# Attention over a small state and a feed-forward block on one core: two weight sums by one group of matmuls, in a newly written order

## The chip, the cores and the metric

The kernel runs on one core of one Trainium2 chip. The engines named here are PE (TensorE, matmul; its weight loads are shown as PEld), DVE (VectorE), ACT (ScalarE), POOL (GpSimd), and SP (SyncE, which here issues most transfers). The time is that of the device for one execution, in microseconds (us).

## The reference

There are eight batches. In each, eight heads of 512 tokens attend to 32 states (and the states to the tokens), and the 512 + 32 rows that result go through a normalisation and a feed-forward block of width 2048 with a residual.

```python
scores = scale * x @ state.T        # softmax over the 32 states
xread  = a @ state                  # 512 rows a batch and head
scores2 = scale * state @ x.T       # softmax over the 512 tokens
sread  = a2 @ x                     # 32 rows a batch and head
x  = concat(xread, sread) with heads joined   # 8 x 544 x 512
xn = (x - mu) / sqrt(var + 1e-6) * g_ln
out = x + max(xn @ w_ch1, 0) @ w_ch2          # 512 -> 2048 -> 512
```

All is float32. The kernel splits each factor into a high and a low float16 part and adds three products of parts (`TERMS`).

## The kernel before

**Front.** The weights come in float64 words and are turned into float32 by `words` (an ACT step, then two DVE steps for each half). `weights1(u)`, for four units of 512 hidden columns, takes the gain and the mean into the first matrix (`means` is line 600, on PE), finds its size, and writes high and low parts (`w1c`). `weights2(u)` does the second matrix (`w2h`). `attention(b)` loads a batch, scales and splits it (`x16`, `sh`), transposes it by transfers of SP (`xT`, `sT`), and makes scores in two PSUM banks named `banks`; ACT takes exponentials of them (`eB`), and DVE transposes them into `ts` for the other softmax. `state_products(b)` multiplies the state with `w1c` (line 666) into `matrix`.

**Batch 0** runs with plain products: `first_products` (line 702) and `second_products_by_unit` (line 716), while the second weights still arrive.

**Batches 1 to 7** use a form of Strassen's scheme with seven products for eight, which is why sums of weight blocks are needed. `sums_of_weights(u)` works by halves of a unit, two a unit, eight in all. In a half it makes four sums: t3 = b22 − b12, b12 = b12 − b11, t2 = b22 − b12 (the new one) and n4 = b21 − t2. Each is four matmuls with plus and minus unit matrices (line 748, `signs`) into a quarter kilobyte of columns, an ACT copy to the high part, and a DVE subtract for the low part. The first two sums go to the left and right half of one PSUM bank (`acc`), the other two to another bank. A bank that is being read by one engine is not written by another: matmuls that come later in the order than a copy out of that bank wait for the copy.

For each batch, two groups of 256 tokens and four units, `strassen_hidden` makes 2 x 256 hidden columns: for block 1 and block 0 each, 12 matmuls (`first`, line 794) into a bank named `half`, of which there are two, and then ACT and DVE steps that take the positive part and form sums (`rs`, `xs`). Block 0's `rs` sums need the values of block 1. POOL makes low parts of the sums. `strassen_products` then issues four runs of matmuls (line 850) that add up in four `acc` banks over the units, and `together` joins them with ACT, DVE and POOL and stores them. The state rows of all batches go last, as a ninth batch with plain first products (line 803).

**What sets the order.** Each of these generators gives a stream, a list of steps. `PLAN` is a string of items `stream:step`, written out by hand as one long table, and `issue` carries the steps out in just that order: every engine has its instructions in the order of the table, and waits are put in by what a step reads and writes. In the profile nearly all steps of ACT, DVE and POOL carry line 187, which is the line of `do` that calls the instruction, so groups are told apart by the names of tiles.

## Time and profile before

| | |
|---|---|
| median of three runs | 695.02 us (693.15 to 695.36) |
| the profiled execution | 693.68 us |
| its span | 691.9 us |
| PE busy | 633.4 us, 92% of the span |
| DVE, ACT, POOL busy | 498.7, 387.9, 215.9 us |
| granted PE clock, mean | 0.977 |

The span runs from the first to the last instruction; 1.8 us of the execution lie around it. Shares are means over unlike stages: in the first 60 us PE is busy less than half, and DVE nearly always; from 180 us on it is the reverse. Rows of the profile read: line, engine, operation, output <- inputs, shapes, count; then busy time, the mean of one in ns, and the idle time of that engine just before these instructions, with what ended it.

### The profile page before, as it was taken

Reading aid. Unit: us, or ns where it says so; the run is one execution under the profiler, and the core shown is the slowest. Engines: PE = TensorE matmul, PEld = TensorE weight load, DVE = VectorE, ACT = ScalarE, POOL = GpSimd, SP = SyncE. Lnnn points to the kernel's source line nnn. Section 1 sums busy time; section 2 is a strip of 40 time slices with the busy share of each in tenths; the row PEclk is TensorE's granted clock in tenths of the full one; section 3 lists DMA queues with packets and bytes.
Section 4 is the critical chain, followed back from the end, with each engine's and each line's share of the span. In section 5 each row is a group of like instructions: output and inputs, shape, how many; then the busy total and the mean of one; then the engine's idle time right before and its main releaser. Section 6 shows DMA issues by size and latency. Waiting matters only on the chain.

```text
span 691.9 us, 14637 instructions
## 1 busy us (share of the span) xinstructions
PE 633.4 (92%) x5945; PEld 494.0 (71%) x5948; DVE 498.7 (72%) x1002; ACT 387.9 (56%) x699; POOL 215.9 (31%) x189
## 2 busy tenths in 40 slices
PE   0648897989998999999999998999999999999996
PEld 0224554546986798778877987688868877889885
DVE  4999886467666676878787777776787687646733
ACT  5498797465654565556555654475456554435332
POOL 0002242330422332533423342433444233423322
PEclk9979898999999999999999999999999999999999
DMA  8898868125340344134213330453223503144221
GB/s 326 273 253 227 245 170 163 24 39 127 95 67 17 81 124 72 38 91 139 58 47 77 95 56 20 101 135 68 64 65 110 105 1 74 39 108 77 63 63 30
DMA packets 98563, 69.63 MB, mean 101 GB/s; under 512 B 72704, under 2 KB 90624, under 8 KB 98048
## 3 DMA queue, kind: packets, MB, share of 16 engines
q1 hardware_dynamic: 96384, 64.77, 36.9%
q0 software_dynamic: 864, 3.15, 2.4%
q8 instruction: 46, 0.75, 0.5%
q10 hardware_dynamic: 1248, 0.79, 0.4%
q14 instruction: 21, 0.17, 0.1%
HBM read 28.05 MB, written 9.44 MB: 54 GB/s over the span
## 4 chain that ended last, share of the span: by engine, by line
PE 74%; DVE 14%; ACT 7%; DMA 2%; issue 2%; POOL 0%; ACTq 0%; DVEq 0%
PE acc L850 34%; PE half L794 18%; PE acc L716 5%; PE half L666 4%; PE half L803 3%; DVE rs L187 2%; PE acc L748 2%; PE acc L702 2%; PE acc L600 2%; ACT xs L187 2%; DVE w_t L187 2%; ACT sums L187 1%; DVE ts L187 1%; ACT eB L187 1%; DMA w1c<-sums 1%
## 5 line engine op out<-in xcount | busy, mean ns | idle before, releaser
L850 PEld LDWEIGHTS <-xs 128*128 128x128 f16 x2520 | 243.2, 98 | 43.3 <-issue 14.0
L187 POOL TENSOR_TENSOR xs<-rs,xs 128x512 f16<-128x512 f32 x120 | 140.3, 1181 | 270.6 <-ACT xs L187 206.9
L850 PE MATMUL acc<-w2h,xs 128*128 128x256 f16 x1440 | 184.1, 274 | 0.0
L794 PE MATMUL half<-ea,matrix 128*128 128x256 f16 x1344 | 162.7, 273 | 6.1 <-DVE matrix L187 2.7
L794 PEld LDWEIGHTS <-matrix 128*128 128x128 f16 x1344 | 130.2, 98 | 26.0 <-issue 8.0
L850 PE MATMUL acc<-sums,xs 128*128 128x256 f16 x1080 | 141.6, 273 | 0.0
L187 DVE SCALAR_TENSOR_TENSOR rs<-half,rs 128x256 f32<-128x256 f32 x224 | 89.9, 419 | 34.4 <-ACT xs L187 14.7
L187 ACT ACTIVATE xs<-half 128x256 f16<-128x256 f32 (+1 forms) x112 | 54.0, 487 | 89.3 <-DVE rs L187 39.0
L187 ACT ACTIVATE xs<-rs 128x512 f16<-128x512 f32 (+1 forms) x128 | 77.6, 619 | 41.3 <-DVE rs L187 37.5
L187 DVE SCALAR_TENSOR_TENSOR xs<-half,xs 128x256 f16<-128x256 f32 (+1 forms) x112 | 61.1, 550 | 32.4 <-ACT xs L187 30.5
L187 ACT ACTIVATE matrix<-half,hs 128x512 f16<-128x512 f32 x56 | 37.7, 684 | 30.4 <-PE half L666 30.2
L187 DVE SCALAR_TENSOR_TENSOR matrix<-half,hs,matrix 128x512 f16<-128x512 f32 x56 | 41.0, 742 | 15.3 <-ACT matrix L187 15.3
L716 PE MATMUL acc<-w2h,hid 128*128 128x512 f16 x192 | 43.1, 379 | 0.0
L187 DVE TENSOR_TENSOR strip<-acc,strip 128x256 f32<-128x256 f32 (+1 forms) x60 | 33.3, 555 | 11.8 <-PE acc L850 8.0
L187 ACT ACTIVATE rs<-half 128x256 f32<-128x256 f32 x56 | 21.3, 380 | 31.2 <-PE half L794 19.4
L666 PE MATMUL half<-w1c,sT 128*32 128x512 f16 x448 | 33.8, 384 | 2.5 <-DVE xs L187 1.2
L716 PEld LDWEIGHTS <-hid 128*128 128x128 f16 x192 | 18.5, 98 | 22.3 <-issue 1.9
L600 PE MATMUL acc<-w_t,gm 128*128 128x512 f32 x32 | 18.2, 725 | 15.7 <-DVE w_t L187 15.7
L187 POOL TENSOR_TENSOR hid<-strip,hid 128x512 f16<-128x512 f32 x16 | 19.8, 1244 | 39.5 <-ACT hid L187 39.4
L187 POOL TENSOR_TENSOR ts<-ts,mA 128x1024 f32<-128x1024 f32 (+1 forms) x8 | 15.4, 1919 | 51.5 <-DVE of_weights L187 30.1
L702 PE MATMUL acc<-ea,matrix 128*128 128x256 f16 x192 | 26.9, 301 | 2.1 <-ACT strip L187 1.1
L187 POOL TENSOR_TENSOR ts<-ts,dA 128x1024 f32<-128x1024 f32 (+1 forms) x8 | 14.4, 1806 | 45.3 <-DVE of_weights L187 23.6
(152 smaller groups left out, 783.0 us busy)
## 6 DMA issues: line engine op xcount, KB each, us to landing
raw<-in_moe_w_ch_dram SPq DMA_DIRECT2D x9, 1024.0 KB, 10.4
out_dram<-xr SPq DMA_DIRECT2D x16, 512.0 KB, 3.2
x_f<-in_x_dram SPq DMA_DIRECT2D x15, 512.0 KB, 5.6
sums<-in_moe_w_ch_dram SPq DMA_DIRECT2D x7, 1024.0 KB, 6.1
ek<-ea SPq DMA_DIRECT2D x56, 64.0 KB, 2.1
ek<-ek SPq DMA_DIRECT2D x7, 512.0 KB, 4.3
xr<-part POOLq DMA_DIRECT2D x6, 512.0 KB, 5.0
w1c<-raw SPq DMA_DIRECT2D x8, 256.0 KB, 4.2
```

Of the source, the lines that this page charges most:

```text
L187: return lambda: f(*map(now, args), **{k: now(v) for k, v in kw.items()})
L600: nc.tensor.matmul(ps, lhsT=gm[:, k:k + 1].broadcast_to([P, P]), rhs=t4[:, k], start=k == 0, stop=k == 3)
L666: nc.tensor.matmul(ps[32 * j:32 * j + 32], lhsT=sT[:, g, a, 32 * j:32 * j + 32], rhs=w[:, 2 * g + j // 2, j % 2], start=a == 0, stop=a == ...
L702: nc.tensor.matmul(o[:, 256 * f:256 * f + 256], lhsT=m[:, g, i, P * (q + f):P * (q + f) + P], rhs=ea[:, s, k, g], start=f == 0 and g == 0 ...
L716: nc.tensor.matmul(po, lhsT=hid[:, i, q, c * P:(c + 1) * P], rhs=w[:, j, q], start=first and q == 0 and n == 0, stop=last and q == 3 and n ...
L748: nc.tensor.matmul(o, lhsT=signs[:, k // 2], rhs=v[k], start=start and k == 0, stop=k == 3, skip_group_check=True)
L794: nc.tensor.matmul(ps[:, 256 * q:256 * q + 256], lhsT=m[:, h, i, P * (2 * k + q):P * (2 * k + q) + P], rhs=ea[:, 0, j, h, 256 * g:256 * g ...
L803: nc.tensor.matmul(ps[:, 256 * q:256 * q + 256].rearrange("p (t n) -> p t n", t=2), lhsT=w[:, k // 2, k % 2, fs] if k < H else wn[:, k - H ...
L850: nc.tensor.matmul(po[o], lhsT=y[:, n, i, o] if o < 2 else x[:, o - 2, n, i], rhs=v[j], start=u == 0 and n == 0 and k == 0 and o in (2, 1, ...
```

## The change

Two things change. `sums_of_weights` issues the first two sums of a half as one group of eight matmuls; then come their two ACT copies and two DVE subtracts. The third and fourth sum are as they were. The number of instructions on each engine stays the same. Second, `PLAN` is a new table: everything is put in a new order. A further stream, `warmth`, has no steps, since `WARM` is 0.

```diff
+WARM = 0
 PLAN = (
-    "1:2 0:0 1:1 1:0 1:3-15 1:24-25 3:1 3:6 3:5 3:7 1:17-18 1:22 3:0 3:3 1:72 3:2 3:4 3:8 2:1 2:6 2:5 1:23 2:7 1:19 "
...
+    "1:0 1:3-4 1:1-2 1:5-12 4:1 1:19 1:72 0:0 4:6 1:20 1:24-25 4:5 4:7 4:0 4:3 1:17-18 4:2 4:4 3:1 3:6 1:22-23 "
...
-            for k, (d, a, b) in enumerate(((t3, b22, b12), (b12, b12, b11), (t2, b22, b12), (n4, b21, t2))):
-                yield do(subtract, k % 2 == 0, o[k], *a, *b)
-                yield do(nc.scalar.activation, d[0], o[k], AF.Copy)
-                yield do(nc.vector.tensor_tensor, d[1], o[k], d[0], ALU.subtract)
+            for pairs in (((t3, b22, b12), (b12, b12, b11)), ((t2, b22, b12),), ((n4, b21, t2),)):
+                first = len(o)
+                def subtract_all(*v, first=first):
+                    for k in range(len(v) // 5):
+                        subtract(first != 1 and k == 0, *v[5 * k:5 * k + 5])
+                todo = [(d, a, b, o.pop(0)) for d, a, b in pairs]
+                yield do(subtract_all, *[v for d, a, b, p in todo for v in (p, *a, *b)])
+                for d, a, b, p in todo:
+                    yield do(nc.scalar.activation, d[0], p, AF.Copy)
+                    yield do(nc.vector.tensor_tensor, d[1], p, d[0], ALU.subtract)
...
+    warm = half()
+
+    def warmth():
+        for _ in range(WARM):
+            yield do(nc.tensor.matmul, warm, lhsT=ones, rhs=ones.unsqueeze(1).broadcast_to([P, 4, P]), start=True, stop=True)
+
+    streams.append(list(warmth()))
```

ACT's order at the first sums (`sums<-acc` and `w2h<-acc` are the copies of a sum out of its bank, `sums,of_weights<-w_t` the sizes of the last second weights; `part` and `strip` belong to batch 0). Before:

```order
L187 ACTIVATE part<-acc,of_unit 128x512 x2
L187 ACTIVATE strip<-acc 128x512
L187 ACTIVATE hid<-strip 128x2x256
L187 ACTIVATE sums<-acc 128x256
L187 ACTIVATE sums,of_weights<-w_t 128x2048
L187 ACTIVATE sums<-acc 128x256
L187 ACTIVATE w2h<-acc 128x256
L187 ACTIVATE sums<-acc 128x256
```

Now:

```order
L186 ACTIVATE w2h<-acc 128x256
L186 ACTIVATE x_401<-x_f,x_s 128x8x64
L186 ACTIVATE sums<-sums 128x1024
L186 ACTIVATE part<-acc,of_unit 128x512 x2
L186 ACTIVATE sums<-acc 128x256
L186 ACTIVATE x_401<-x_f,x_s 128x8x64
L186 ACTIVATE part<-acc,of_unit 128x512
L186 ACTIVATE sums,of_weights<-w_t 128x2048
L186 ACTIVATE strip<-acc 128x512 x2
```

The first half's two copies (here the second sum's first) now stand ahead of the sizes, with other work between them; before, the second sum of the next half came behind the sizes.

DVE's order at the softmax of batch 2, before:

```order
L187 SCALAR_TENSOR_TENSOR xs<-half,xs 128x2x256
L187 SCALAR_TENSOR_TENSOR rs<-half,rs 128x256 x3
L187 TENSOR_REDUCE mB<-banks 128x2
L187 SCALAR_TENSOR_TENSOR xs<-half,xs 128x2x128
L187 TENSOR_SCALAR mB<-mB,es 128x2
L187 STREAM_TRANSPOSE ts<-banks 128x1024
L187 SCALAR_TENSOR_TENSOR matrix<-half,hs,matrix 128x512
L187 TENSOR_REDUCE mA<-ts 128x32
```

Now:

```order
L186 SCALAR_TENSOR_TENSOR xs<-half,xs 128x2x128
L186 TENSOR_SCALAR es<-x_i 128x1
L186 STREAM_TRANSPOSE ts<-banks 128x1024
L186 SCALAR_TENSOR_TENSOR rs<-half,rs 128x256 x3
L186 SCALAR_TENSOR_TENSOR xr<-strip,of_second,xr 128x512
L186 SCALAR_TENSOR_TENSOR rs<-half,rs 128x256
L186 SCALAR_TENSOR_TENSOR xs<-half,xs 128x2x256
L186 TENSOR_REDUCE mB<-banks 128x2
L186 TENSOR_SCALAR mB<-mB,es 128x2
L186 TENSOR_REDUCE mA<-ts 128x32
```

The transpose `ts<-banks` moved from behind the maxima `mB` (and so behind the exponentials that need them) to ahead of them.

ACT's order in a hidden step of batch 2, with the numbers of the tiles (`half` with the shape 128x2x256 is block 0; 128x256 and 128x2x128 are block 1). Before:

```order
L187 ACTIVATE xs_2746<-half_2724 128x2x128
L187 ACTIVATE rs_2761<-half_2724 128x256
L187 ACTIVATE xs_2746<-half_2748 128x2x256
L187 ACTIVATE xr_2786<-banks_2769,ux_2109 128x1024
L187 ACTIVATE xs_2746<-rs_2761 128x4x128 x2
```

Now:

```order
L186 ACTIVATE xs_2723<-half_2710 128x2x256
L186 ACTIVATE xs_2666<-rs_2633 128x4x128
L186 ACTIVATE rs_2740<-half_2727 128x256
L186 ACTIVATE xs_2723<-half_2727 128x2x128
L186 ACTIVATE xs_2723<-rs_2740 128x4x128 x2
```

Block 0 is now made and read first, and its bank `half_2710` is read again by the `rs` sums once block 1 has been read. In 22 of the 60 hidden steps block 0 comes first now; in 6 of 60 before.

240 rows, old and new, of the table PLAN are left out of this document.

## The prediction

> **What bounds the kernel now.** I read the head and the chain of waits of the profile page first:
>
> ```profile
> span 691.9 us, 14637 instructions
> PE 633.4 (92%) x5945; PEld 494.0 (71%) x5948; DVE 498.7 (72%) x1002; ACT 387.9 (56%) x699; POOL 215.9 (31%) x189
> PE 74%; DVE 14%; ACT 7%; DMA 2%; issue 2%; POOL 0%; ACTq 0%; DVEq 0%
> ```
>
> TensorE (PE) is busy for 633.4 us of 691.9. The change issues the same matmuls, so it can win or lose only in the other 58.5 us and in the time that matmuls take under a lower clock. Where the idle time lies is told by the view of windows (us of the stretch, then busy time and instructions of PE, weight loads, DVE, ACT and POOL, then granted PE clock, DMA share, GB/s):
>
> ```profile
> 0.00:60.00 60.00, 29.17 (x184) 12.96 (x187) 47.86 (x87) 37.22 (x51) 2.80 (x8) 0.89 0.91 276
> 60.00:100.00 40.00, 35.64 (x281) 22.39 (x280) 35.64 (x67) 35.16 (x50) 12.44 (x10) 0.91 0.73 202
> 100.00:160.00 60.00, 52.05 (x340) 28.82 (x339) 38.23 (x67) 39.03 (x66) 18.61 (x16) 0.94 0.42 91
> 160.00:180.00 20.00, 19.53 (x208) 15.45 (x207) 14.54 (x39) 12.51 (x30) 2.27 (x2) 1.00 0.63 159
> 180.00:680.00 500.00, 491.15 (x4888) 409.40 (x4886) 358.77 (x742) 263.07 (x505) 176.82 (x151) 1.00 0.31 72
> 680.00:692.00 12.00, 5.87 (x54) 5.01 (x52) 3.65 (x6) 0.93 (x2) 2.94 (x3) 0.93 0.16 44
> ```
>
> Idle PE time is 30.8 us before 60, 4.4 in 60 to 100, 7.95 in 100 to 160, 0.5 to 180, 8.85 in the 500 us after that, and 6.1 at the end. So the front is where time lies open; the seven batches behind it run PE at 98%. The groups by line say what ended those gaps (busy us, mean ns, then idle before it and its releasers):
>
> ```profile
> L600 PE MATMUL acc<-w_t,gm 128*128 128x512 f32 x32 | 18.2, 725 | 15.7 <-DVE w_t L187 15.7
> L748 PE MATMUL acc<-w2h,signs 128*128 128x256 f16 x112 | 17.3, 288 | 8.4 <-ACT sums L187 4.4 <-DVE sums L187 4.0
> L794 PE MATMUL half<-ea,matrix 128*128 128x256 f16 x1344 | 162.7, 273 | 6.1 <-DVE matrix L187 2.7 <-DVE xs L187 2.1 <-DVE rs L187 0.9
> L666 PE MATMUL half<-w1c,sT 128*32 128x512 f16 x448 | 33.8, 384 | 2.5 <-DVE xs L187 1.2 <-DVE rs L187 1.1
> L850 PE MATMUL acc<-w2h,xs 128*128 128x256 f16 x1440 | 184.1, 274 | 0.0
> ```
>
> The final products (L850) never wait. The mean-taking matmuls (L600) wait 15.7 us for DVE to make weight words, the block sums (L748) 8.4, and the hidden products and state products (L794, L666) 8.6 for one of the two `half` banks. These three rows are what a new order can touch.
>
> **Term A, the merged sums.** Before, each of eight halves takes four turns of a group of four matmuls, an ACT copy and a DVE subtract; now the sums t3 and b12, which share a PSUM bank, are one group of eight. Matmuls, copies and subtracts stay in number (128, 32, 32), so nothing in busy time moves. What goes is a wait inside the bank. The timeline of PE before shows it (start, length, last the idle time and its releaser):
>
> ```profile
> 112.25 1.36 PE L702 MATMUL acc<-ea,matrix 128*128 128x256 f16 x11
> 113.46 0.60 PE L748 MATMUL acc<-w2h,signs 128*128 128x256 f16 x4
> 117.48 1.87 PE L748 MATMUL acc<-w2h,signs 128*128 128x256 f16 x8 [3.42 <-ACT sums L187]
> 119.82 1.01 PE L748 MATMUL acc<-w2h,signs 128*128 128x256 f16 x4 [0.47 <-ACT sums L187]
> 120.62 2.77 PE L702 MATMUL acc<-ea,matrix 128*128 128x256 f16 x12
> 130.91 0.60 PE L748 MATMUL acc<-w2h,signs 128*128 128x256 f16 x4 [1.58 <-DVE sums L187]
> 149.32 0.60 PE L748 MATMUL acc<-w2h,signs 128*128 128x256 f16 x4 [2.41 <-DVE sums L187]
> ```
>
> and the timeline of ACT, why the first is so long:
>
> ```profile
> 114.82 0.37 ACT L187 ACTIVATE sums<-acc 128x256 f16<-128x256 f32 x1
> 115.16 1.91 ACT L187 ACTIVATE sums<-w_t 128x2048 bf16<-128x2048 f32 x1
> 117.07 0.36 ACT L187 ACTIVATE sums<-acc 128x256 f16<-128x256 f32 x1
> ```
>
> The first sum was in its bank at about 114; ACT reached its copy at 117.07, behind the 1.91 us of weight sizes, and the second group, whose matmuls go to the other half of that bank, stood behind that copy. I laid the written order beside these times: each of the four waits (3.42 + 0.47 + 1.58 + 2.41 = 7.88) is a second sum behind the copies of the first. The same four are nearly all of the 7.95 us that PE idles in 100 to 160. As one group both sums lie in the bank before anyone reads it, so this wait cannot occur again; late copies then delay only their own readers: the third sum, which needs the new b12, and the products much later. The ACT order in the change puts the 1.91 us of sizes behind the first such copy (the rows above the prediction), which leaves the third and fourth sums and the banks as the next to be late. There are four `acc` banks, and a later copy holds one longer; at the rate of one group per 1.36 to 2.8 us of other matmuls the next free bank comes about when it is wanted. I take −7.0: the 8.4 less 1.4 for new, short waits of the later sums, three like the 0.47 row. Bounds: −8.4 (all), and −4.4 (only the share that the row puts on ACT, if the DVE lateness shows again at the next reader).
>
> **Term B, the clock behind that gap.** The same PE rows show matmuls at half speed behind the 3.42 us gap: 12 of L702 took 2.77 where 11 took 1.36 before it.
>
> ```profile
> 116.70:123.60 6.90, 5.65 (x28) 3.50 (x31) 1.18 (x3) 1.61 (x6) 0.28 (x1) 0.52 0.46 90
> ```
>
> The granted clock there is 0.52. The loss is 2.77 − 12 × 0.124 = 1.28 on L702, 1.87 − 2 × 0.60 = 0.67 and 1.01 − 0.60 = 0.41 on L748: 2.4 us. Without the gap it isn't paid. I take −2.0, bounds −2.4 and 0 (if another gap as long stands elsewhere in the new order). [...]
>
> **Term C, the order in the batches.** There, three gaps are worth naming; the largest:
>
> ```profile
> 214.64 1.47 PE L794 MATMUL half<-ea,matrix 128*128 128x256 f16 x12
> 216.85 1.25 DVE L187 STREAM_TRANSPOSE ts<-banks 128x1024 f32<-128x1024 f32 x1 [2.88 <-ACT eB L187]
> 218.03 0.71 DVE L187 SCALAR_TENSOR_TENSOR matrix<-half,hs,matrix 128x512 f16<-128x512 f32 x1
> 218.79 2.20 PE L794 MATMUL half<-ea,matrix 128*128 128x256 f16 x12 [2.02 <-DVE matrix L187]
> 220.78 2.46 PE L850 MATMUL acc<-w2h,xs 128*128 128x256 f16 x12
> ```
>
> DVE's transpose of the scores stood 2.88 us for ACT's two exponentials on the same two banks, and behind it in DVE's order stood the `matrix` subtract that frees the `half` bank of the next product. PE paid 2.02, and then 2.20 − 1.47 = 0.73 and 2.46 − 1.47 = 0.99 at the lower clock: 3.7 us. In the new order of batch 2 the transpose stands ahead of the exponentials. Against this, the transpose in batch 4 now stands behind them, which it did not. The rest is how much PE work lies between two uses of a `half` bank. Its release takes, from these rows,
>
> ```profile
> L187 ACT ACTIVATE xs<-half 128x512 f16<-128x512 f32 x56 | 33.2, 594 | 47.9 <-DVE rs L187 24.1 <-PE half L794 18.5 <-PE acc L850 3.8
> L187 DVE SCALAR_TENSOR_TENSOR rs<-half,rs 128x256 f32<-128x256 f32 x224 | 89.9, 419 | 34.4 <-ACT xs L187 14.7 <-ACT rs L187 12.6 <-PE half L794 4.6
> L187 DVE SCALAR_TENSOR_TENSOR xs<-half,xs 128x512 f16<-128x512 f32 x56 | 38.3, 685 | 17.6 <-ACT xs L187 17.6
> ```
>
> for the second-written block three `rs` steps and one `xs` step of DVE, 3 × 0.42 + 0.69 = 1.95, with the 0.59 of ACT ahead 2.5 us. Pricing the matmuls that lie between two uses in the written orders by the means above, 21 of 174 reuses had under 2.5 us of cover and 11 have it now (under 3 us: 35, now 25). By that ratio half of the 8.6 us of waits would go, −4; but 22 of 60 hidden steps, before 6, now compute the block first whose values depend on the other one, so that its bank is held longer, and nothing in the trace prices that at 16 more places. I take −2, the middle of −8 (all 8.6 gone but for the odd one) and +4 (half as much again as there is).
>
> **Term D, the front.** Its end is set by DVE, not by PE:
>
> ```profile
> 7.75 0.17 DVE L187 TENSOR_SCALAR gm<-gx 128x4 f32<-128x4 f32 x1 [5.91 <-DMA gx<-in_moe_g_ln_dram]
> 18.03 4.50 PE L600 MATMUL acc<-w_t,gm 128*128 128x512 f32 x6 [7.12 <-DVE w_t L187]
> 21.23 1.87 SPq L187 DMA_TRANSPOSE sT<-sh  x1
> 41.27 5.68 PE L600 MATMUL acc<-w_t,gm 128*128 128x512 f32 x8 [8.61 <-DVE w_t L187]
> 60.00:80.00 20.00, 16.01 (x162) 11.40 (x161) 19.69 (x39) 19.13 (x27) 6.47 (x5) 0.90 0.91 255
> ```
>
> The move of `gm` off the head of DVE's order lets the work on x start before the 5.91 us wait for gx is over. I followed the chain through the new order with these durations: about 1.5 us earlier for the scale of x; two weight loads swap places, so that the third mean (41.27) can come 2 to 3 us earlier; the transposed x and state are issued behind more of the weights' DVE work, sT at about 22.4 for 21.2, and SP's next weight load, queued behind that transpose, 1.4 us later. Up to the first product DVE has 59.3 us of work ahead of it, before 54.6; up to the first product of the second half of batch 0 both have 99.8. Since DVE is busy 19.69 of 20 us in 60 to 80, a shuffle of equal work there can't win much. I take 0, with −4 (gx and the mean both pass through) and +5 (the 4.7 us more DVE work ahead of the first product stays).
>
> **Term E, a short cover.** One final product of batch 1 now has 1.8 us of work between the steps that make its inputs and itself (2.46 at least before); L850, which waited 0.0, may wait there. +1, bounds 0 and +2. The tail (6.1 us idle in the last window) has the same steps in both, DVE's strips and the last stores: 0.
>
> **The sum.** −7 − 2 − 2 + 0 + 1 = −10. The profiled execution took 693.68 us (span 691.9 and 1.8 around it), so the changed kernel, profiled, should take about 683.7. The median of the three runs shown, 695.02, lies 1.34 above the profiled one; with that, **685 us**.
>
> **The rivals.**
>
> *Nothing gained.* The gaps of 100 to 160 are only where PE meets a front that ACT and DVE feed; close them and PE waits for the next weights instead. For it: ACT and DVE are each busy 35 of 40 us in 60 to 100. Against it: in 160 to 180 PE is busy 19.53 of 20, so work was ready behind the sums, and the feeding engines are busy only 39 and 38 of 60 us in 100 to 160. Time: A and B fall away, C and E nearly cancel: 694.
>
> *Slower by the held banks.* If each of the 16 more steps with the dependent block first holds its bank over the other block's group and its first ACT and DVE steps (1.47 + 0.38 + 0.42 = 2.3 us) and 1.3 of that shows, it costs 16 × 1.3 = 21 us; with A, B, and E, −8 + 21 = +13, less the 4 of the shorter covers: +9, 704. It decides from the point where less than 2.5 us of other PE work lies behind such a pair. Against it: by the written order every such pair but one has 2.6 us or more behind it.
>
> *Slower by the front.* The first product comes 4.7 us later, and with it everything; the sums then find ACT still as busy and A is worth nothing: −2 + 5 + 1 = +4, 699. For it speaks the 19.69 of 20; against it that the work ahead of the second half is equal.
>
> *More than forecast.* The front's 2 to 3 us come through and all of the `half` waits go: A −8.4, B −2.4, C −8, D −3 gives −22, and half of C's remainder lost again, −18: 677.
>
> **How the numbers follow.** Forecast 0.50, nothing gained 0.14, held banks 0.10, late front 0.08, more than forecast 0.18. A change under 0.3% (2.1 us, what the three runs' spread lets one tell) counts as none: that is 692.9 to 697.1. Faster: 0.50 + 0.18 and a small share of "nothing gained", 0.70. Slower: 0.10 + 0.08 = 0.18. Same: 0.12. The forecast's own range by the bounds of A to E, not all at their ends, is 679 to 690. For 8 in 10 I reach down to 675, past most of the large gain, and up to 698, over "nothing gained" and a part of the late front.
>
> **What would show it.** A: the group of L748 (new line) with idle under 2 us in place of 8.4, and PE busy over 57 of 60 us in 100 to 160 of the new profile, or wherever the sums then lie. B: no stretch of clock near 0.5 around the sums. C: idle before L794 and L666 together near 6, no DVE transpose that waits near 3 us in batch 2. D: the first wait of DVE no longer for gx, the third mean near 38 to 39, the first product no later than before. If idle before L794 and L666 is over 15, the held banks decided; if the first products of batch 1 begin later than before, the front did. The forecast is wrong above all if PE's idle time before 180 stays near 43.6 us though the sums no longer wait.

## The result, and the profile after

The changed kernel takes 667.86 us (median of four runs, 667.4 to 668.16); the kernel before, run beside it, 694.85 (693.15 to 695.36). The ratio is 0.9615, with a 95% interval of 0.9597 to 0.9633: 27 us faster, where the prediction had 10 and a range down to 675.

The head of the page and the chain of waits after:

```profile
span 665.9 us, 14680 instructions
PE 626.3 (94%) x5948; PEld 493.1 (74%) x5948; DVE 498.0 (75%) x1002; ACT 388.2 (58%) x699; POOL 216.7 (33%) x189
PE 90%; DVE 5%; DMA 2%; ACT 1%; issue 1%; DVEq 0%; SPq 0%
```

The span is 26.0 us shorter. DVE, ACT and POOL do what they did, to within 1 us. PE's busy time fell by 7.1 us, though its matmuls are the same, and its idle time by 18.9 (58.5 to 39.6); what the 7.1 are is worked out under term B below. The chain that ended last now lies on PE for 90%, before for 74%. Where the idle time went is told by windows cut alike in both. Before:

```profile
0.00:100.00 100.00, 64.81 (x462) 35.34 (x466) 83.49 (x152) 72.37 (x100) 15.24 (x18) 0.90 0.84 246
100.00:180.00 80.00, 71.58 (x546) 44.27 (x545) 52.77 (x105) 51.54 (x95) 20.89 (x18) 0.96 0.48 108
180.00:660.00 480.00, 471.15 (x4705) 391.47 (x4703) 351.51 (x728) 255.96 (x492) 172.32 (x147) 1.00 0.32 73
```

After:

```profile
0.00:100.00 100.00, 68.12 (x502) 38.37 (x503) 84.07 (x154) 74.13 (x104) 15.00 (x19) 0.90 0.83 247
100.00:180.00 80.00, 80.00 (x655) 53.80 (x654) 59.14 (x129) 58.96 (x112) 25.07 (x22) 1.00 0.51 106
180.00:660.00 480.00, 478.12 (x4795) 400.88 (x4793) 352.72 (x717) 255.13 (x484) 176.63 (x148) 1.00 0.31 75
```

Idle time of PE (the stretch less the first busy time): 35.2 to 31.9 in the first 100 us, 8.4 to 0.0 from there to 180, 8.85 to 1.9 in the batches to 660. That is 3.3 + 8.4 + 7.0 = 18.7. With the 7.1 of busy time and 0.2 at the end it makes the 26.0. The groups of PE say the same by line (the lines of the changed file; L599 is L600 of before, L747 L748, L799 L794, L665 L666, L855 L850):

```profile
L599 PE MATMUL acc<-w_t,gm 128*128 128x512 f32 x32 | 18.0, 719 | 6.7 <-DVE w_t L186 6.7
L747 PE MATMUL acc<-w2h,signs 128*128 128x256 f16 x112 | 15.4, 273 | 0.0
L799 PE MATMUL half<-ea,matrix 128*128 128x256 f16 x1344 | 159.4, 273 | 0.0
L665 PE MATMUL half<-w1c,sT 128*32 128x512 f16 x448 | 33.5, 384 | 1.9 <-DVE rs L186 1.0 <-DVE xs L186 0.9
L855 PE MATMUL acc<-w2h,xs 128*128 128x256 f16 x1440 | 183.0, 273 | 0.0
```

The sums wait for nothing any more (8.4 before), the hidden products for nothing (6.1), the state products 1.9 (2.5). The part of PE's timeline with the first merged group (two sums), and the row of ACT's first copy out of its bank:

```profile
102.41 1.04 PE L747 MATMUL acc<-w2h,signs 128*128 128x256 f16 x8
103.69 7.94 PE L715 MATMUL acc<-w2h,hid 128*128 128x512 f16 x36
```

```profile
107.08 0.38 ACT L186 ACTIVATE w2h<-acc 128x256 f16<-128x256 f32 x1
```

The copy comes 3.6 us after the sums are in the bank, and PE goes on with 36 other matmuls meanwhile: ACT is as late as before, and no matmul stands behind it.

### The profile page after: what moved, and what is told of

Same layout as the page of the kernel before. It is cut to its first block, busy times and chain, and to the rows that moved or that the text cites. A ratio compares the mean times of both kernels' runs of the same rounds, so it can differ in the third digit from the quotient of the medians.

```text
span 665.9 us, 14680 instructions
## 1 busy us (share of the span) xinstructions
PE 626.3 (94%) x5948; PEld 493.1 (74%) x5948; DVE 498.0 (75%) x1002; ACT 388.2 (58%) x699; POOL 216.7 (33%) x189
## 4 chain that ended last, share of the span: by engine, by line
PE 90%; DVE 5%; DMA 2%; ACT 1%; issue 1%; DVEq 0%; SPq 0%
PE acc L855 41%; PE half L799 22%; PE acc L715 6%; PE half L665 5%; PE acc L701 3%; PE half L808 3%; PE acc L747 2%; PE acc L599 2%; PE banks L403 1%; DVE w_t L186 1%; PE banks L479 1%; PE banks L515 1%; PE banks L492 1%; DMA x_f<-in_x_dram 1%; PE acc L608 1%; DMA w1c<-raw 1%
## 5 line engine op out<-in xcount | busy, mean ns | idle before, releaser
L855 PEld LDWEIGHTS <-xs 128*128 128x128 f16 x2520 | 242.4, 98 | 43.6 <-issue 15.3
L186 POOL TENSOR_TENSOR xs<-rs,xs 128x512 f16<-128x512 f32 x120 | 142.4, 1199 | 272.7 <-ACT xs L186 207.1
L855 PE MATMUL acc<-w2h,xs 128*128 128x256 f16 x1440 | 183.0, 273 | 0.0
L799 PE MATMUL half<-ea,matrix 128*128 128x256 f16 x1344 | 159.4, 273 | 0.0
L799 PEld LDWEIGHTS <-matrix 128*128 128x128 f16 x1344 | 130.7, 98 | 16.6 <-issue 0.8
L855 PE MATMUL acc<-sums,xs 128*128 128x256 f16 x1080 | 141.9, 273 | 0.0
L186 ACT ACTIVATE xs<-rs 128x512 f16<-128x512 f32 x128 | 77.1, 618 | 40.5 <-DVE rs L186 33.8
L186 ACT ACTIVATE matrix<-half,hs 128x512 f16<-128x512 f32 x56 | 38.0, 687 | 35.2 <-PE half L665 34.9
L665 PE MATMUL half<-w1c,sT 128*32 128x512 f16 x448 | 33.5, 384 | 1.9 <-DVE rs L186 1.0
L186 DVE SCALAR_TENSOR_TENSOR x<-x_f,x_s,x 128x512 f16<-128x512 f32 x32 | 24.8, 798 | 5.3 <-ACT x L186 5.3
L186 DVE BATCH_NORM_STATS2 s<-xr 128x6 f32<-128x512 f32 x32 | 21.6, 684 | 8.7 <-ACT xr L186 8.6
L186 ACT ACTIVATE x<-x_f,x_s 128x512 f16<-128x512 f32 x32 | 21.7, 713 | 9.8 <-DVE x_s L186 9.8
```

The lines of the kernel that those rows point to most:

```text
L186: return lambda: f(*map(now, args), **{k: now(v) for k, v in kw.items()})
L665: nc.tensor.matmul(ps[32 * j:32 * j + 32], lhsT=sT[:, g, a, 32 * j:32 * j + 32], rhs=w[:, 2 * g + j // 2, j % 2], start=a == 0, stop=a == ...
L799: nc.tensor.matmul(ps[:, 256 * q:256 * q + 256], lhsT=m[:, h, i, P * (2 * k + q):P * (2 * k + q) + P], rhs=ea[:, 0, j, h, 256 * g:256 * g ...
L855: nc.tensor.matmul(po[o], lhsT=y[:, n, i, o] if o < 2 else x[:, o - 2, n, i], rhs=v[j], start=u == 0 and n == 0 and k == 0 and o in (2, 1, ...
```

## The experiments

In each experiment the change's code and both tables are the material; `merged` below means the change's `sums_of_weights` with the steps of its streams (19 to 22) renumbered in the old table. Line numbers of PE's matmuls and of the helper differ by a few from file to file. The kernel before took 694.2 to 694.7 us beside these runs.

### Which part of the change brings how much

Four kernels put the change together piece by piece. The merging alone, in the old order:

```diff
-    "15:0 7:23 19:12 7:39 19:15 17:25 14:9-10 14:1"
+    "15:0 7:23 19:11 7:39 17:25 14:9-10 14:1"
```

(stream 19 is the sums of unit 0; old steps 12 and 15 are the two groups of a half, new step 11 is the group of eight), and so for the other seven halves.

> The order of before throughout, with only the first two sums of each half made by one group of eight matmuls, where the first sum's group stood. Theory (each place pays for itself): the 8.4 us that PE waited at L748 go, and the 2.4 us of lower clock behind the longest wait: 694.9 - 10.8 = 684 us, and PE idle at the sums near 0. Rival (the order does it, the merging does nothing): the copies are as late as before, so the third sum, which needs the new b12, takes over the wait, and less than 4 us go: 691 us or more, with an idle time at L747 of over 4 us.

Measured: 681.55 us, ratio 0.982 (0.9792 to 0.9848), 12.6 us faster. In its profile, the page's head, the sums' group, and the stretch of the sums:

```profile
span 679.4 us, 14636 instructions
PE 628.1 (92%) x5945; PEld 491.9 (72%) x5948; DVE 498.2 (73%) x1002; ACT 387.1 (57%) x699; POOL 215.7 (32%) x189
L752 PE MATMUL acc<-w2h,signs 128*128 128x256 f16 x112 | 15.2, 273 | 0.0
100.00:180.00 80.00, 79.95 (x664) 53.43 (x662) 59.36 (x122) 57.93 (x111) 26.36 (x23) 1.00 0.49 113
```

All 8.4 us of waiting at the sums are gone, with the old order's late copies left as they were, and the third sum did not take the wait over: the rival falls. The span is 12.5 us shorter. Idle time makes 7.2 of that (58.5 to 51.3): of the 8.4, 0.8 came back in the first 100 us, ahead of the sums, and 0.3 in the batches. Busy time makes 5.3 (633.4 to 628.1). Of that 2.4 is the lower clock behind the 3.42 us gap. Another 1.7 was not foreseen: this kernel still has the 2.02 us gap of batch 2, and the clock behind it stayed up.

```profile
207.97 1.47 PE L804 MATMUL half<-ea,matrix 128*128 128x256 f16 x12 [2.02 <-DVE matrix L191]
```

The same gap of the same length had cost the clock before (2.20 us for these 12 matmuls). The last section puts that down to where the gap fell, not to the merging; less these 1.7 us the merging is worth about 11, an estimate from this one trace.

The merging with the new order up to the first sums, the old one after it (here and in the next three diffs the rule stands by which the table was made; the kernel has the table itself):

```diff
+head = [step for step in NEW[:395] if step in OLD[:395]]
+PLAN = head + [step for step in OLD if step not in head]
```

(389 steps; `OLD` has the sums' steps renumbered.)

> The merged sums; the new order for the first 389 steps of the table (the weights, the attention of batch 0 and the greater part of batch 0's products, up to about 114 us of before), the old order for what follows. Theory: the front's PE idle time fell by 3.3 us in the change, and that passes through, so 3 to 4 us under the run with the merging alone. Rival (a front that is fed by DVE and ACT gives its gain back at the sums): the same time as the merging alone, within 1 us.

Measured: 688.42 us, ratio 0.9922 (0.9895 to 0.9949): 6.9 us slower than the merging alone, which neither theory had. The trace shows a wait that belongs to the seam and to neither order:

```profile
124.43 1.05 PE L408 MATMUL banks<-xT,sT 128*32 128x512 f16 x8 [8.75 <-DMA xT<-x]
```

The new front does the work on batch 1's x at other places than the old rest expects it, so the scores wait 8.75 us for their transposed x. The run says nothing of the front's worth.

The new order up to the last sum and the old order in the batches, and the reverse (both with the merging):

```diff
+PLAN = NEW[:665] + [step for step in OLD if step not in NEW[:665]]
```

> The new order up to the last weight sum (665 steps, about 182 us of before), the old order in the batches after it. Theory: the change's waits in the batches (8.85 us of PE idle time fell to 1.9, and about 2 us of lower clock went) are missing here, so about 9 us over the change's 667.9: 677 us. Rival (the front sets all, and the batches' waits come from a late start): within 3 us of 667.9.

```diff
+PLAN = OLD[:665] + [step for step in NEW if step not in OLD[:665]]
```

> The merged sums, the old order up to the last weight sum, the new order in the batches. Theory: about 9 us under the run with the merging alone, which adds to the front's and the sums' part to make the whole 27. Rival (the parts overlap): 4 us or less under the merging alone.

Measured: 678.12 us for the first (ratio 0.977, 0.9744 to 0.9796) and 671.89 for the second (0.9675, 0.9642 to 0.9707). The new batches are worth 681.55 − 671.89 = 9.7 us on the old front, and 678.12 − 667.86 = 10.3 on the new one. The new front and sums are worth 681.55 − 678.12 = 3.4 with old batches, and 671.89 − 667.86 = 4.0 with new ones. So the parts add up to nearly the 27: 12.6 for the merging, about 10 for the batches, 3.4 to 4.0 for the rest. The windows of both show where (first the one with old batches, then the one with the old front):

```profile
0.00:100.00 100.00, 67.60 (x500) 38.40 (x504) 84.04 (x154) 74.59 (x104) 15.27 (x20) 0.90 0.85 249
180.00:660.00 480.00, 471.21 (x4695) 391.67 (x4694) 347.56 (x712) 251.76 (x481) 169.95 (x144) 1.00 0.31 74
```

```profile
0.00:100.00 100.00, 63.77 (x455) 35.09 (x459) 81.84 (x151) 71.09 (x98) 15.24 (x18) 0.91 0.82 244
180.00:660.00 480.00, 478.12 (x4796) 401.09 (x4794) 354.41 (x723) 257.89 (x490) 174.55 (x146) 1.00 0.31 74
```

With the new front PE has been busy 3.8 us more by 100 us; with the new batches it is busy 6.9 us more in 480. To split the 3.4 to 4.0 between the front and the order of the sums' stretch, I ran the old front with everything else new:

```diff
+head = [step for step in OLD[:395] if step in NEW[:395]]
+PLAN = head + [step for step in NEW if step not in head]
```

> The change with the old order for the first 389 steps (the weights, attention and greater part of batch 0's products, to about 114 us), the merged sums, and the new order from there on, the sums' stretch too. The old front with the sums' stretch of before measured 671.9. Theory (the remaining 4 us are the front's, whose PE idle time to 100 us fell by 3.3): 671 to 672 us, as there. Rival (they are the order of the sums' stretch, and the front gives nothing): within 1 us of 667.9.

Measured: 674.26 us, ratio 0.9698 (0.9672 to 0.9724), slower than either had it. Again the seam makes waits of its own, with ACT:

```profile
130.71 2.75 PE L718 MATMUL acc<-w2h,hid 128*128 128x512 f16 x12 [1.17 <-ACT part L189]
135.13 1.03 PE L750 MATMUL acc<-w2h,signs 128*128 128x256 f16 x8 [1.67 <-ACT part L189]
```

Less these 2.8 us it would be at 671.4, like the old front with the old sums, which speaks for the front; but an order that is cut at 114 us costs by the cut alone. PE's rows speak for the front too: in the traces with the new front the second products of batch 0 begin at 82.5 to 84.7 us, behind 394 to 397 matmuls, with the old front at 85.0 to 87.3, behind 382 to 385. What the order of the sums' stretch adds is not separated.

### Does the new order still need the merging?

```diff
-    "11:2 19:11 10:11"
+    "11:2 19:12 10:11"
...
-    "14:1-2 19:14 17:24"
+    "14:1-2 19:13 19:15-16 17:24"
```

The sums are two groups of four again (new step 11 becomes old step 12, and old step 15, the second group, stands right behind the first group's ACT copy, old step 13), in the new order.

> The new order with the first two sums of a half as two groups of four again, the second one put right behind the copy of the first, as in before. Theory (the merging is needed: every second sum waits for a turn on the bank): 3 to 8 us slower than the change, 671 to 676 us, with idle time before the sums. Rival (the new order puts the copies where ACT and DVE are in time, the merging adds nothing): within 1.5 us of 667.9.

Measured: 673.53 us, ratio 0.9696 (0.9676 to 0.9716), 5.7 us slower than the change. The sums' group has its idle time again, and two rows of PE's timeline show the turns:

```profile
L750 PE MATMUL acc<-w2h,signs 128*128 128x256 f16 x112 | 16.5, 272 | 4.9 <-ACT sums L189 4.9
107.14 0.60 PE L750 MATMUL acc<-w2h,signs 128*128 128x256 f16 x4 [1.48 <-ACT sums L189]
122.59 0.60 PE L750 MATMUL acc<-w2h,signs 128*128 128x256 f16 x4 [0.47 <-ACT sums L189]
```

The theory holds: a second sum that has to wait for its turn costs 0.6 to 1.7 us (by the starts of the matmuls, 6.1 in all), seven times out of eight, in the new order too. In the old order the merging was worth 12.6, here 5.7: the new order alone saves about a third of the waits (by the starts of the matmuls 9.4 us in before, 6.1 here), and the clock behind the long one.

### The batches: what makes the half banks late

On the run with the merging alone, two DVE steps moved:

```diff
-    "41:37 33:2 41:39 42:3-4 34:13 34:4 41:40-42 41:38 42:5"
+    "41:37 33:2 41:38-39 42:3-4 34:13 34:4 41:40-42 42:5"
...
-    "95:0 101:41 96:8 101:46 96:3 96:7"
+    "95:0 101:41 96:8 96:3 96:7"
...
-    "98:3 98:7 101:47"
+    "98:3 98:7 101:46-47"
```

(41:38 is the transpose of batch 2's scores, 41:39 the maxima; 101:46 the 2-element addition of batch 5.)

> The run with the merging alone (681.5 us) with two DVE steps moved and nothing else: in the softmax of batch 2 the transpose of the scores goes ahead of the maxima (it stood behind both exponentials, and PE idled 2.02 us behind it), and in the softmax of batch 5 the 2-element addition to the sums goes some ten steps later (it took 1.77 us where it usually takes 0.16, ending 20 ns after a POOL instruction, and PE idled 1.80 and 0.34 us behind it). Theory (the waits in the batches come from single DVE steps that are held up, by ACT or by POOL, with the release of a half bank queued behind them): both gaps go, 2.0 + 2.1 = 4.1 us, 677.4 us. Rival (the banks are short of cover in any case, another step is late at the same place): less than 1.5 us, 680 us or more.

Measured: 678.01 us, ratio 0.9764 (0.9738 to 0.9789), 3.5 us faster than without the moves; expected 4.1. Where the 2.02 us gap was, the next hidden product now follows the 0.82 us of matmuls between without idle time:

```profile
203.60 1.47 PE L804 MATMUL half<-ea,matrix 128*128 128x256 f16 x12
205.57 1.47 PE L804 MATMUL half<-ea,matrix 128*128 128x256 f16 x12
```

In batch 5 the wait of 1.80 is gone too, but 0.5 of it came back later in the batch, behind ACT. So two single steps in DVE's order made about a third of what the batches lost. I then moved five more groups of DVE steps behind releases of half banks:

```diff
-    "61:53-54 56:1 61:55 61:45 56:3 53:3 56:2 56:4"
+    "56:1 61:45 56:3 53:3 56:2 56:4 61:53-55"
...
-    "81:43 71:9 81:44-45 82:12 74:14 74:12 75:1 82:13-14"
+    "81:43 71:9 82:12 74:14 74:12 75:1 82:13-14 81:44-45"
...
-    "101:44-45 95:1 96:2 96:4"
+    "95:1 96:2 96:4 101:44-45"
...
-    "101:53-54 95:2 98:0 96:12 98:5 98:2 98:4"
+    "95:2 98:0 96:12 98:5 98:2 98:4 101:53-54"
...
-    "121:53-54 118:0 118:2 118:4"
+    "118:0 118:2 118:4 121:53-54"
```

(Steps 44 are the low parts of the exponentials, 45 their transposing transfer, 53 and 54 the addition and the reciprocal of the softmax's sums, 55 POOL's product with them; 56, 82, 98 and 118 are the half-bank steps that go ahead.)

> The run with the merging and two moves (678.0 us), with five more groups of DVE steps moved behind the steps that free a half bank: the sums of the softmax (an addition and a reciprocal, 0.5 us) in batches 3, 5 and 6, and the low part of the exponentials (1.23 us) in batches 4 and 5, where PE idled 1.0, 1.3, 1.6, 0.6 and 0.5 us. Theory (each idle time of PE in the batches is one such step ahead of the release of a half bank): 0.5 us each at the three, 0.6 and 0.5 at the two, 2.6 us in all, 675.4 us. Rival (the releases are late for the matmuls, ACT or cover, and not for the steps ahead): less than 1 us, 677 us or more.

Measured: 679.37 us, ratio 0.9775 (0.9752 to 0.9798), no better than before the five moves (1.4 slower). The theory fails as a rule. Two of the five did what they should (in batch 6 1.22 us of idle time became 0.67, in batch 5 0.51 went); the gap of batch 4 and the next one of batch 5 grew. DVE's and PE's rows in batch 5:

```profile
416.13 1.73 DVE L191 SCALAR_TENSOR_TENSOR eb<-eB,eb 128x1024 f16<-128x1024 f32 x1
420.25 0.61 PE L670 MATMUL half<-w1c,sT 128*32 128x512 f16 x8 [1.85 <-DVE rs L191]
420.80 2.24 PE L860 MATMUL acc<-w2h,xs 128*128 128x256 f16 x12
```

The low part that had stood ahead of one release now stands ahead of the next, and at its new place takes 1.73 us where it took 1.23. PE idles 1.85 us instead of 1.12, and this time the clock fell as well (2.24 us for 12 matmuls that take 1.47). From 180 to 660 us PE idles 0.3 us less than before the five moves, and PE's 3.41 us at half clock cost 1.7: that is the 1.4. So a DVE step ahead of a release is one cause; a release that comes late because several engines' steps follow each other closely is another, and a step that is moved by hand falls on the next release.

On the change itself, two places were left in the batches where PE idles. There I moved four steps:

```diff
-    "61:46 55:2 55:0 61:43 56:8 41:75 61:47 56:11 61:44-45 56:6 56:10 55:1 56:9 61:50 56:2 56:4"
+    "55:2 55:0 61:43 56:8 41:75 56:11 56:6 56:10 55:1 56:9 61:44-45 61:50 56:2 56:4 61:46-47"
...
-    "121:34-35 100:8 116:2 116:4"
+    "121:34 100:8 116:2 116:4 121:35"
```

> The change with DVE steps moved at the two places where PE still idles in its batches (about 1.1 us each, near 274 and 473): in the softmax of batch 3 the two small steps on the sums and the low part of the exponentials go behind the steps that free the half bank, in batch 6 the low part of the state's copy goes behind one. Both held DVE up while a POOL instruction ran (1.71 us for a 2-element step, 2.18 us for one of 0.75). Theory (a DVE step of this kind waits for POOL's instruction to end, and the bank's release stands behind it): both gaps go, 665.5 to 666.5 us. Rival (something else is late by as much): 667.5 or more.

Measured: 665.36 us (664.49 to 666.74), ratio 0.9589 (0.9565 to 0.9614): 2.5 us faster than the change, and the fastest of all. In the change, at the second place, POOL, DVE and PE:

```profile
470.60 1.91 POOL L186 TENSOR_TENSOR ts<-ts,mA 128x1024 f32<-128x1024 f32 x1 [2.15 <-DVE mA L186]
470.88 2.18 DVE L186 SCALAR_TENSOR_TENSOR sk<-s_r,x_s,sk 64x512 f16<-64x512 f32 x1
473.57 0.62 PE L665 MATMUL half<-w1c,sT 128*32 128x512 f16 x8 [0.92 <-DVE xs L186]
```

With the step moved:

```profile
469.56 0.42 DVE L190 SCALAR_TENSOR_TENSOR xs<-half,xs 128x256 f16<-128x256 f32 x1 [0.51 <-ACT xs L190]
470.01 1.24 DVE L190 SCALAR_TENSOR_TENSOR sk<-s_r,x_s,sk 64x512 f16<-64x512 f32 x1
470.78 0.61 PE L669 MATMUL half<-w1c,sT 128*32 128x512 f16 x8
```

The step `sk` still ends 0.54 us behind POOL's instruction, as it did in the change, but it now stands behind the release; PE's matmul no longer waits, and the gap at the first place (0.96 us) is gone too. So the theory holds for both places. Their worth is smaller than the 2.5: of the 2.6 us between the two profiled spans 1.4 lie ahead of the first moved step, where the orders are the same. The first product starts at 63.98 us here and at 65.36 in the change; in other traces with this front it starts as late as 66.19. That lead is not the moves'; they are worth about 1.3 in these two traces.

The prediction feared block 0 ahead of block 1. In eleven of the places where the change does that I swapped the two back (one of them):

```diff
-    "61:31-32 49:0-1 47:14"
+    "61:31-32 49:5 49:1 47:14"
...
-    "61:9 61:7 49:5 47:11-12"
+    "61:9 61:7 49:0 47:11-12"
```

> The change with block 1 first again in 11 of the 19 hidden steps of batches 1 to 7 where it made block 0 first (the two groups swapped, and their first ACT steps where needed). Theory (which block is first does not matter as long as the cover is there): within 1.5 us of 667.9. Rival of the prediction (block 0 first holds its bank longer and costs): at least 2 us faster, 666 us or less. Third (block 0 first is part of the gain): at least 2 us slower, 670 or more, with idle time before the hidden products.

Measured: 668.47 us, ratio 0.9618 (0.9599 to 0.9637): the same as the change, with 0.0 idle before the hidden products in both. Which block comes first neither costs nor gains here.

### The front and the clock

```diff
+    "175:0-15 4:8"
...
+    "175:16-24 3:14"
...
+    "175:25-28 1:73"
...
+    "175:29-35 6:9"
...
+    "175:36-40 1:90"
```

(stream 175 is the change's `warmth` with `WARM = 41`; the items behind it are the PE steps that it goes ahead of.)

> The change with 41 matmuls that nobody reads, put into five idle times of PE in the front (9 to 16, 28 to 33, 39 to 42, 54 to 57 and 62 to 63 us). Theory (the clock's fall behind these idle times costs on the way to the products; the front's matmuls that ran slow, about 2 us in the first two groups of means and 2 us at 57 to 67, get faster): 1 to 3 us faster, 665 to 667 us, with a granted clock of over 0.95 in 20 to 68 us. Rival (the front is DVE's and the transfers', PE's slow matmuls there are hidden): within 0.7 us of 667.9. Third (an added matmul is in the way of a real one): slower by 1 us or more.

Measured: 668.52 us, ratio 0.9633 (0.9606 to 0.9661), no gain. The change's window from 20 to 40 us, and the same with the added matmuls:

```profile
20.00:40.00 20.00, 14.35 (x61) 5.91 (x59) 18.40 (x32) 11.72 (x13) 0.00 (x0) 0.83 1.00 321
20.00:40.00 20.00, 13.14 (x68) 5.50 (x69) 19.53 (x36) 12.89 (x13) 0.00 (x0) 1.00 1.07 321
```

The clock is up, and the whole takes as long: DVE was and is busy for 18 to 19.5 of the 20 us. The first product starts 1.1 us sooner than in the change (64.27 for 65.36, within the spread of this front), and PE then waits 1.38 us for ACT and 1.09 for DVE, so that the second products start at 84.17 for 83.82. In this trace the slow clock of the front is hidden.

```diff
-    "1:72 0:0 4:6"
+    "1:72 4:6"
...
-    "1:0 1:3-4"
+    "0:0 1:0 1:3-4"
```

> The change with the small step on the gains at the head of DVE's order again, where it waits for its transfer until 7.75 us, as in before; nothing else. Theory (the front's gain is the work on x that starts 1.25 us earlier): 1 to 1.5 us slower, 669 to 669.5 us. Rival (the front's gain lies in the order of weights, the start of x is hidden behind the first weights' arrival): within 0.7 us of 667.9.

Measured: 668.66 us, ratio 0.9639 (0.9615 to 0.9662), 0.8 us slower than the change, between the two expectations. The two intervals overlap, and its first product (65.93) lies within the spread of the front, so this is not told from nothing. The wait for the gains is at most a small part of the 3.4 to 4.0.

The four moves and the 41 matmuls together:

> The moves in batches 3 and 6 and the 41 matmuls in the front together. By the first theories of the two runs alone: 663 to 665.5 us, the sum of the two; by the rivals 667 to 668.

Measured: 667.78 us, ratio 0.9618 (0.9595 to 0.9642), 2.4 us slower than the moves alone. The gaps in the batches are gone as there. The profiled execution loses in the front: the first product starts as early as with the moves alone (64.02 for 63.98), then PE waits 1.95 us for ACT, and from 77.50 to 80.92 the clock is at half, so that 36 matmuls take 5.94 us where they take 4.11. The second products start at 85.83 for 82.46. With the added matmuls alone that clock did not fall; why it fell here is not shown.

The last experiment measures the clock by itself, with idle times of PE made to order in the batches:

```diff
+            one, two = half(), half()
+            yield do(nc.tensor.matmul, one, lhsT=ones, rhs=row, start=True, stop=True)
+            yield do(nc.scalar.activation, scratch, one, AF.Copy)
+            for _ in range(n - 1):
+                yield do(nc.scalar.activation, scratch, scratch, AF.Copy)
+            yield do(nc.tensor.matmul, two, lhsT=scratch[:, 0:P], rhs=row, start=True, stop=True)
```

> The change with 16 idle times of PE put into the batches: a matmul, one to five ACT copies of about 0.6 us each of its result, and a matmul that needs the last copy; the output stays as it is. The sizes are about 1.0, 1.6, 2.2, 2.8 and 3.4 us, most of them 1.6 to 2.8. It measures by itself after which idle time the granted clock falls. Theory of the prediction (an idle time of about 2 us lowers the clock, as behind the 2.02 us in before): it falls after all 2.2 us ones. [...] Time: 667.9 + 16 x about 2.5 + some 2 for each fall: 705 to 735 us.

Measured: 763.29 us, once. My sizes were off: the first matmul also waits for a half bank, so that most idle times are two, with one matmul of 0.2 us between. Two of the sixteen, as PE's timeline has them:

```profile
211.55 0.38 PE L191 MATMUL half<-ones 128*128 128x512 bf16 x1 [1.84 <-DVE matrix L191]
213.28 0.39 PE L191 MATMUL half<-ones,scratch 128*128 128x512 bf16 x1 [1.35 <-ACT scratch L191]
213.51 0.71 PE L860 MATMUL acc<-w2h,xs 128*128 128x256 f16 x5
519.98 0.39 PE L191 MATMUL half<-ones 128*128 128x512 bf16 x1 [0.65 <-DVE rs L191]
524.39 0.61 PE L191 MATMUL half<-ones,scratch 128*128 128x512 bf16 x1 [4.02 <-ACT scratch L191]
524.79 2.77 PE L860 MATMUL acc<-w2h,xs 128*128 128x256 f16 x12
```

Behind 1.84 + 1.35 us the matmuls keep their pace (5 in 0.71); behind 0.65 + 4.02 twelve take 2.77 in place of 1.47. Over all sixteen the clock fell behind the twelve with 3.31 us or more of idle time in both parts together, and stayed up behind four (1.35, 2.12, 2.72 and 3.19 us). A fall made 11 to 27 matmuls slow and cost 1.3 to 3.0 us (half of PE's busy time at half clock). The theory, that 2 us are enough, doesn't hold in general. But it isn't a plain threshold on the length of a gap either: the single gap of 2.02 us lowered the clock in before and in the two runs with the new front and old batches, and did not in the run with the merging alone. The last section sets the idle times beside the times at which the granted clock changes.

## Why the prediction was right or wrong

The direction and the largest mechanism were right; the size was not, and the time lies outside the range. Of the 27 us the merging made 12.6 (terms A and B had 9), the batches about 10 (C had 2) and the front with the sums' order 3.4 to 4.0 (D and E had a loss of 1).

**What bounds the kernel, and the places.** Right: the idle time that the three rows named (the sums, the half banks, the means) is what fell, 8.4 to 0.0, 8.6 to 1.9 and 15.7 to 6.7 (of the last, little reached the end). Wrong: that a change can win only in the 58.5 us of idle time and in the lower clock. Some 3 us of waiting stood in the busy time, as term B shows.

**Term A (−7.0; the waits of second sums).** Right, at its outer bound: −8.4 of idle time. I held back 1.4 for new waits of the later sums and banks, and there were none: 0.0 at L747 in the change, and 0.0 with the old order too. That PE and not the feed of the weights set the time there, the prediction read from 160 to 180 us; the merging alone confirmed it, and "nothing gained" fell.

**Term B (−2.0; the lower clock behind the longest wait).** Behind the sums it was 2.4 as worked out, but PE's busy time fell by 7.1 in all. The clock is the larger part. From 100 us on, before had two stretches at half clock, the one behind the sums,

```profile
116.97:123.80 6.83, 5.85 (x32) 3.50 (x31) 1.18 (x3) 1.54 (x6) 0.01 (x1) 0.50 0.45 87
```

and one of 3.41 us behind the 2.02 us gap, in which PE was busy throughout. The change has none until its last 4 us. Half of 5.85 + 3.41 is 4.6 us. The rest is an estimate: 12 matmuls of 256 columns take 1.47 us, one every 0.11, but the last one before a gap counts as busy for its full 0.27. So each gap hides about 0.16 us in the busy time, and by PE's rows from 100 us on before has 22 gaps of over 20 ns at full clock and the change 3: 19 × 0.16 = 3.0. Together that is 7.6, near the 7.1. The step that failed is the price of a gap: I counted its idle time, and the lower clock behind one of them; a second fall of the clock (1.7) stood in C only, where it was halved with the rest, and what the gaps hide in the busy time stood nowhere.

**Term C (−2; the batches).** The step that failed most: −2 where the hybrids have 9.7 to 10.3. On the old front that is 7.3 of idle time (9.2 to 1.9 from 180 to 660 us) and about 2 that 13 fewer gaps leave in the busy time; on the new front the 1.7 us of lower clock behind the 2.02 us gap come on top. The list of places was right, and so was the reading of the 2.02 us gap, whose cause (the transpose behind the exponentials) the two moves showed. What was wrong is the middle of −8 and +4. I had counted that reuses with little cover fell from 21 to 11, and then took half of the gain away again for block 0 standing first in 16 more steps, an effect that no row showed; eleven of them undone changed nothing. And in weighing the waits by a count of covers I let 11 short covers stand for half the waits, when 0.0 us remained before the hidden products: a short cover is a risk, not a wait.

**Term D (0; the front).** Off by 3.4 to 4.0 us, with the order of the sums' stretch, at the end of its range (−4). The details read from the order came true or nearly: no wait for gx at the head, the third mean at 35.08 for 41.27 (6.2 us earlier; I had 2 to 3), and the first product later by what DVE had more ahead of it, as PE's rows show, before and then after:

```profile
59.72 2.79 PE L702 MATMUL acc<-ea,matrix 128*128 128x256 f16 x24
```

```profile
65.36 1.89 PE L701 MATMUL acc<-ea,matrix 128*128 128x256 f16 x8
```

5.6 us later (I had 4.7 of DVE work), and yet the front gained. The step that failed is the measure: I took the first product for the point from which the front counts. In the new order PE starts later and then hardly stops; by 100 us it has been busy 3.3 us more. How much of the 3.4 to 4.0 is the front's, and how much the sums' order's, is open.

**Term E (+1).** 0: L855 waited 0.0, as before.

**The rivals.** Held banks: fell (0.0 before L799, and the swap of eleven). Late front: the first product was late as it said, and the time that it drew from that was wrong. More than forecast, −18: the right side, and still 9 short, because it gave back half of what the half banks free, had no second fall of the clock in B, and nothing for what gaps hide in the busy time.

**The range.** The bounds of A to E at their good ends make −8.4 − 2.4 − 8 − 4 + 0 = −22.8, 4 us short of what came; the range went down to −20 of that, since I thought the good ends would not all meet. The hybrids show that the parts do not hinder each other, and each came at its good end or past it: A with B at 12.6 for 10.8, C at about 10 for 8, D at 3.4 to 4.0 for 4.

## What to carry to other kernels

Two results that share a PSUM bank are best written by one run of matmuls before anyone reads: the second one then has no turn to wait for, and here it did not matter that the readers were over 3 us late (about 11 us without the chance of the clock in the old order, 5.7 in the new). Where PE is busy for 98%, look at each gap of a microsecond for the single DVE or ACT step that stood ahead of a bank's release, and count as part of the gap's price what it hides in the busy time (0.16 us here) and, where it is long, the matmuls that run slow behind it (1.3 to 3.0 us a time in the experiment with idle times made to order). Gains of an order add up between stages that are each complete, but a step that is moved by hand, or a seam between two orders, makes new waits at once: look at the trace of each such move before counting on it.

## What the runs showed of the hardware

**DVE steps that wait for POOL.** A step of two elements (`rB<-sumB`) took 1.77 us in before and 1.71 in the change where it takes 0.16 undisturbed. Before, on POOL and then DVE:

```profile
426.25 1.92 POOL L187 TENSOR_TENSOR ts<-ts,mA 128x1024 f32<-128x1024 f32 x1 [4.37 <-DVE mA L187]
426.42 1.77 DVE L187 TENSOR_SCALAR rB<-sumB 128x2 f32<-128x2 f32 x1
```

It ends when POOL's instruction ends, at 428.2. In the two traces some 30 DVE steps each take over 0.1 us longer than others of their kind, 16 to 20 us together in each, while a POOL instruction runs or has just ended; the small ones end 20 to 30 ns after it. The long ones have all operands in SBUF (`rB`, `sk`, `eb`, `x_i` are among them): of the steps of that sort that overlap a POOL instruction, 29 of 115 are long in before and 32 of 131 in the change. Of those that read a PSUM bank, none is, of 247 and of 238; the `rs<-half` steps are an example, of which in before 83 of the 224 overlap a POOL instruction and none takes over 0.43 us (the mean is 0.42). Why some steps in SBUF are long and others are not, the traces do not tell. Here even a step of two elements did not end before POOL's instruction had ended.

**The clock after a gap.** The length of a gap alone does not tell here whether the clock falls; with its place it does, from 100 us on. In each of the sixteen traces the times at which the granted clock changes lie whole multiples of 3.41 us apart, and the stretches at half clock from 100 us on last 3.41 or 6.83, but for the one that the end of the trace breaks off. I drew marks 3.41 us apart through these times in each trace and added up PE's idle time between each two of them. Divided at its marks, before has around the 2.02 us gap

```profile
215.95:219.37 3.42, 1.40 (x14) 1.10 (x12) 2.52 (x3) 1.42 (x6) 0.59 (x1) 1.00 0.00 0
219.37:222.78 3.41, 3.41 (x19) 2.41 (x17) 1.91 (x6) 1.75 (x3) 1.91 (x1) 0.50 0.02 5
```

and the run with the merging alone, where a mark falls into the same gap,

```profile
203.74:207.16 3.42, 2.21 (x21) 1.84 (x19) 1.12 (x1) 2.81 (x8) 1.16 (x1) 1.00 0.00 0
207.16:210.57 3.41, 2.60 (x24) 2.32 (x24) 2.68 (x6) 1.09 (x2) 1.44 (x1) 1.00 0.02 5
```

In the first the whole 2.02 us lie in one stretch, and the next one runs at 0.50. In the second 1.20 lie on one side and 0.82 on the other, and the clock stays up. In before and the change there are 332 stretches at full clock from 100 us on: half clock follows the three in which PE idles 2.02, 2.37 and 2.91 us, and none of the others, which idle 1.80 us or less. It is the same in all sixteen traces: of 2669 such stretches, half clock follows each of the 34 with 1.85 us or more of idle time, and none of the others, which have 1.80 or less. The 3.19 us of idle time made to order that left the clock up were divided by a mark into 1.49 and 1.70. Counted from the start of the span, the first mark lies differently in each of these traces (0.91 us in before, 0.25 in the change, 2.35 in the run with the merging alone), and the mean clock of one kernel differs between its executions (0.976 to 0.981 for before). So idle times of 1.85 to 3.19 us cost the clock in some places here and not in others, and by these counts it went with where the marks fell. In the front, from 60 to 100 us, idle time alone does not tell: in before half clock followed a stretch with 1.17 us of it (at 72.59), and did not follow one with 1.24 (at 62.35); why is open.
